# One wait ahead of a batch's DMA transposes, and two rectifications one slot later, in a fused attention and expert-layer kernel

## Chip, cores, metric

One core of one Trainium2 chip. The metric is the device time of one execution in microseconds (us), lower is better. The profile is one execution that the hardware profiler recorded; its span is about 1.7 us shorter than the time that the same execution is given (986.4 against 988.07 us for the kernel before). A run also has its mean *granted clock*: the share of full speed that the throttle allowed TensorE (PE).

## The reference, cut

Linear attention with cosine re-weighting, whose output goes through a router with eight rounds of balancing and eight experts.

```python
def phi(x, c, s):                      # c, s: cos and sin by position
    r = np.maximum(x, 0.0)
    return np.concatenate([r * c, r * s], axis=-1)
q_p, k_p = phi(q, ...), phi(k, ...)    # q, k, v: (8 batches, 8 heads, 576, 64)
kv  = einsum('bhsf,bhsd->bhfd', k_p, v);  z = k_p.sum(2)
num = einsum('bhsf,bhfd->bhsd', q_p, kv)
den = einsum('bhsf,bhf->bhs', q_p, z) + 1e-06
x   = (num / den)                      # then 4608 tokens x 512
# ... router, 8 rounds of balancing P, then for each of 8 experts:
out += P[:, e:e+1] * (np.maximum(x @ w1[e], 0) @ w2[e])
```

## The kernel before: the parts that matter

Expert 0 works on *blocks* of 512 tokens. A block has 16 *slots*: in slots 0 to 7 PE makes one part each of `h_ps` (x times w1), in slots 8 to 15 half a tile each of `y_ps` (h times w2). The attention of the coming batches is slipped in between: block `j` attends batch `j+1` and prepares batch `j+2`. Batches are counted from 0, so "the fourth batch" is `b == 3`, prepared in block 1. Each batch has four head pairs `hk`.

```python
ld      = tc.tile_pool(name="ld", bufs=4)        # q, k, v as loaded
qp_pool = tc.tile_pool(name="qp_pool", bufs=3)   # q_p before it is turned
ps_s    = tc.tile_pool(name="ps_s", bufs=4)      # small products, in PSUM
# ...
def load(b, half, names="qkv", held_back=False):
    for name in names:
        i = nc.gpsimd.dma_start(out=x, in_=...)  # 288 KB, two head pairs; float32 to fp16
        if held_back:
            after(ve.last, i)                    # not before what DVE was last given
        # ...
def prep_k(b, hk, by_scalar=True):               # rectifies k: ACT, in place
    se.activation(out=k16, in_=k16, func=AF.Relu)
def prep_q(b, hk):                               # b >= 2
    ve.tensor_scalar(out=q16, in0=q16, scalar1=0.0, op0=ALU.max)
    q_p = qp_pool.tile([P, C, 2, D], F16, name="q_p")
    ve.tensor_tensor(out=q_p, in0=q16, in1=cs, op=ALU.mult)
    nc.sync.dma_start(out=qTs[b, hk], in_=q_p, transpose=True)   # SyncE's queue
def prep_kv(b, hk):                              # DVE: k_p, then the copy of v
# ...
def attend(b, hk):       # PE: rb_ps; ACT: rb = copy(rb_ps); PE: num_ps; DVE: xT = num_ps * rb
# ... block 1 (j == 1), slot by slot:
#   0: loads of batch 3: second half of q, both of k, both of v (held back)
#   9, 10, 12, 13: attend(2, 0..3)
for slot, fn, hk in (                            # preparation of batch 3
    (4, prep_q, 0), (5, prep_q, 1), (7, prep_k, 0), (8, prep_q, 2),
    (8, prep_k, 1), (10, prep_kv, 0), (10, prep_k, 2), (12, prep_q, 3),
    (12, prep_kv, 1), (12, prep_k, 3), (13, prep_kv, 2), (14, prep_kp, 3),
    (14, prep_v, 3),
): ...
#   12: all six loads of batch 4 (held back);  15: key-value sums of batch 3, first half
#   block 2, slot 0: second half of those sums; slot 3: denominators, which need all four
#   transposed q of batch 3
```

PE, VectorE (DVE) and ScalarE (ACT) each work in written order, so an instruction that waits holds back everything behind it on its engine. The loads come from GpSimd's queue, the transposes from SyncE's.

## Time and profile before

| | before |
|---|---|
| time, median of 4 runs | 987.33 us (986.19 to 987.55) |
| profiled span, mean granted clock | 986.4 us, 0.996 |
| PE busy | 969.7 us, 98% |
| last `v` load of batch 3, issue to landing | 14.6 us |
| transposes of batch 3, issue to landing | 14.4, 15.1, 8.2, 3.2 us |
| PE idle from 57 to 70 us (waits with a releaser) | 4.5 us |

The page of the kernel before: the span, the engines' busy time, then three of its rows of 40 slices of 24.7 us each (PE's busy tenths, the granted clock, DMA's busy tenths).

```profile
span 986.4 us, 20270 instructions
...
PE 969.7 (98%) x7871; PEld 675.6 (68%) x7871; DVE 806.9 (82%) x1834; ACT 564.4 (57%) x1262; POOL 60.7 (6%) x82
...
PE   9989999989999999999999999999999999999997
...
PEclk9989999999999999999999999999999999999999
DMA  9999890642013410133113400133103401104535
...
```

PE is the bound nearly everywhere; the third slice (49 to 74 us) is the one in the attention part where PE shows an 8 and the granted clock an 8. In that slice DMA is at 9.

The waits of the kernel before, from 55 to 70 us: engine, line, tile, what it waited for, then us in total, times, longest.

```profile
...
engine line waited for: us in total, times, longest us
...
ACT k_ld L109 <- DMA k_ld<-in_k_dram: 6.6, 2, 4.9
DVE acc_lo L109 <- DMA v_ld<-in_v_dram: 5.1, 1, 5.1
PE small_ps L109 <- ACT rb L109: 4.1, 2, 3.0
...
```

ACT stood 4.9 us at a rectification whose `k` had not landed, DVE 5.1 us at a copy of `v`. Neither is PE, but PE writes its small products into four PSUM buffers (`ps_s`), and before the fourth attend those of the third come free only when ACT has copied `rb_ps` out, behind that rectification, and when DVE has made `xT`, behind that copy.

PE's timeline of the kernel before: start, us, instruction, and in brackets the idle time before it and what ended it.

```profile
...
start us, us, engine line op out<-in xcount [idle before <-releaser]
...
59.45 0.46 PE L109 MATMUL small_ps<-hl,acc_hi 96*128 96x192 f16 x3 [1.07 <-ACT rb L109]
...
62.96 1.04 PE L109 MATMUL y_ps<-w2e,hT 128*128 128x512 f16 x4
67.02 0.64 PE L109 MATMUL small_ps<-hl,acc_hi 96*128 96x192 f16 x3 [3.02 <-ACT rb L109]
68.05 0.69 PE L109 MATMUL small_ps<-q_pT,kv_sb 128*64 128x384 f16 x4 [0.39 <-DVE xT L109]
68.68 3.59 PE L109 MATMUL y_ps<-w2e,hT 128*128 128x512 f16 x8
72.20 1.17 PE L109 MATMUL small_ps<-acc_lo,k_p 64*128 64x65 f16 x36
...
74.50 0.74 PE L109 MATMUL small_ps<-acc_lo,k_p 64*128 64x65 f16 x36
...
```

The second attend waits 1.07 us, the fourth 3.02. After that gap the same work takes longer: eight `y_ps` matmuls take 3.59 us (1.90 elsewhere), 36 small ones 1.17 (0.74).

Why longer is in the view by windows: busy time of PE, weight loads, DVE, ACT and GpSimd, then the granted clock, the DMA share and GB/s.

```profile
...
core 0: us, PE busy (x) PEld busy (x) DVE busy (x) ACT busy (x) POOL busy (x), PEclk, DMA share, GB/s
64.00:67.00 3.00, 0.00 (x0) 0.00 (x0) 0.00 (x0) 1.57 (x4) 0.00 (x0) 0.99 1.31 135
67.00:70.00 3.00, 2.59 (x11) 1.14 (x11) 2.89 (x7) 2.42 (x6) 0.00 (x0) 0.50 1.09 154
70.00:74.00 4.00, 4.00 (x45) 1.85 (x44) 3.02 (x8) 1.02 (x3) 3.39 (x5) 0.53 0.80 104
...
```

From 64 to 67 us PE did nothing; from 67.0 to 73.8 its clock was half. The chain that ended last (start, us, what) runs through one load here:

```profile
...
53.23 13.82 DMA v_ld<-in_v_dram
...
67.45 0.56 DVE xT L109
...
68.05 0.69 PE small_ps L109 x4
...
```

### The profile page before, as it was taken

The numbers are of one execution on the slowest core, as the hardware profiler recorded it, in microseconds if no ns is written. First come the engines' busy times: TensorE is split into PE (matmuls) and PEld (weight loads), VectorE is DVE, ScalarE is ACT, GpSimd is POOL, SyncE is SP. The second block draws the span as 40 slices with busy tenths as digits, with TensorE's granted clock in tenths as the row PEclk, the third lists the DMA queues.
The fourth block names the chain that finished last, engine by engine and source line by source line (L and its number), as shares of the span: only waits on it lengthen the run. The fifth ranks groups of instructions, "written<-read, shape, count | busy, mean of one in ns | idle before, by whom it ended". The sixth has DMA issues, their size and how long they took to land.

```text
span 986.4 us, 20270 instructions
## 1 busy us (share of the span) xinstructions
PE 969.7 (98%) x7871; PEld 675.6 (68%) x7871; DVE 806.9 (82%) x1834; ACT 564.4 (57%) x1262; POOL 60.7 (6%) x82
## 2 busy tenths in 40 slices
PE   9989999989999999999999999999999999999997
PEld 6534545447777777777777777777777777777775
DVE  7766774789889888988789888988789888988887
ACT  5746665467776555555555555555555555555551
POOL 6222110010000000000000000000000000000001
PEclk9989999999999999999999999999999999999999
DMA  9999890642013410133113400133103401104535
GB/s 163 186 129 165 150 153 21 127 74 60 26 49 68 78 38 25 42 75 68 45 29 67 92 25 26 51 65 68 49 25 67 92 25 27 48 26 116 129 86 129
DMA packets 80336, 73.54 MB, mean 75 GB/s; under 512 B 33264, under 2 KB 72176, under 8 KB 80240
## 3 DMA queue, kind: packets, MB, share of 16 engines
q0 software_dynamic: 27232, 30.94, 20.3%
q1 hardware_dynamic: 52768, 41.06, 17.2%
q8 instruction: 61, 1.00, 0.4%
q14 instruction: 35, 0.29, 0.1%
q10 hardware_dynamic: 240, 0.26, 0.1%
HBM read 83.12 MB, written 12.98 MB: 97 GB/s over the span
## 4 chain that ended last, share of the span: by engine, by line
PE 90%; DMA 5%; issue 2%; DVE 2%; POOL 1%; ACT 1%; POOLq 0%; DVEq 0%; ACTq 0%; SPq 0%
PE rows_ps L109 34%; PE h_ps L109 27%; PE copied_ps L109 11%; PE p_ps L109 11%; PE y_ps L109 4%; PE small_ps L109 3%; DMA v_ld<-in_v_dram 1%; DMA w1e<-in_moe_w_dram 1%; DMA w2e<-in_moe_w_dram 1%; DMA k_ld<-in_k_dram 1%; POOL q_ld L201 0%; DVE acc_hi L922 0%; POOL hs_last L937 0%; DVE P_tok L109 0%; DMA out_dram<-acc_lo 0%
## 5 line engine op out<-in xcount | busy, mean ns | idle before, releaser
L922 DVE SCALAR_TENSOR_TENSOR acc_lo<-rows_ps,P_tok,acc_lo 128x512 f32<-128x512 f32 (+1 forms) x322 | 203.3, 640 | 74.4 <-PE rows_ps L109 74.3
L109 PEld LDWEIGHTS <-H 128*128 128x128 f16 x2080 | 203.0, 98 | 83.1 <-issue 1.2
L858 ACT CAST u<-h_ps 128x384 f16<-128x384 f32 x288 | 137.6, 478 | 131.2 <-PE h_ps L109 131.2
L109 PEld LDWEIGHTS <-w1e 128*128 128x128 f16 x1632 | 156.5, 98 | 66.6 <-issue 6.5
L852 DVE CUSTOM_DVE_ANT_0 H<-p_ps,u 128x384 f16<-128x384 f32 x329 | 181.1, 550 | 6.9 <-PE p_ps L109 6.5
L109 PEld LDWEIGHTS <-hs 128*128 128x128 f16 x1500 | 146.5, 98 | 56.2
L109 PE MATMUL h_ps<-S,w1e 128*128 128x384 f16 x672 | 164.1, 326 | 1.1 <-ACT u L109 0.9
L109 PE MATMUL p_ps<-xT,T 128*128 128x384 f16 x672 | 164.1, 326 | 0.1
L109 PE MATMUL rows_ps<-V,H 128*128 128x256 f16 x1000 | 150.0, 273 | 0.7 <-DVE acc_hi L922 0.7
L109 PE MATMUL h_ps<-xT,w1e 128*128 128x384 f16 (+1 forms) x616 | 150.2, 351 | 0.1
L109 PE MATMUL rows_ps<-w2e,hs 128*128 128x256 f16 x1000 | 150.0, 273 | 0.0
L890 ACT ACTIVATE H<-h_ps 128x384 f16<-128x384 f32 x144 | 70.6, 490 | 95.1 <-PE h_ps L109 95.1
L109 PEld LDWEIGHTS <-T 128*128 128x128 f16 x1008 | 98.1, 98 | 29.3 <-issue 2.8
L109 PE MATMUL rows_ps<-w2e,H 128*128 128x256 f16 (+1 forms) x568 | 91.2, 285 | 0.0
L871 ACT COPY copied_ps<-h_ps 128x384 f32<-128x384 f32 x144 | 67.5, 469 | 35.3 <-PE h_ps L109 35.3
L881 ACT ACTIVATE H<-copied_ps 128x384 f16<-128x384 f32 x144 | 70.9, 492 | 20.4 <-PE copied_ps L109 20.4
L109 PE MATMUL h_ps<-S,T 128*128 128x384 f16 x336 | 81.8, 325 | 0.3 <-ACT copied_ps L109 0.3
L109 PE MATMUL copied_ps<-xT,w1e 128*128 128x384 f16 x336 | 82.1, 326 | 0.0
L109 PE MATMUL copied_ps<-w2e,H 128*128 128x256 f16 x504 | 75.5, 272 | 0.0
L109 PE MATMUL rows_ps<-V,hs 128*128 128x256 f16 x500 | 74.9, 272 | 0.0
L922 DVE SCALAR_TENSOR_TENSOR acc_lo<-copied_ps,P_tok,acc_lo 128x256 f32<-128x256 f32 x126 | 60.1, 477 | 0.4
L922 DVE SCALAR_TENSOR_TENSOR acc_hi<-rows_ps,P_tok,acc_hi 128x512 f32<-128x512 f32 (+1 forms) x56 | 41.3, 737 | 20.5 <-PE rows_ps L109 19.7
(147 smaller groups left out, 953.5 us busy)
## 6 DMA issues: line engine op xcount, KB each, us to landing
S<-x_saved SPq DMA_DIRECT2D x108, 192.0 KB, 2.4
out_dram<-acc_lo SPq DMA_DIRECT2D x62, 128.0 KB, 2.4
w1e<-in_moe_w_dram POOLq DMA_DIRECT2D x7, 1024.0 KB, 9.1
w2e<-in_moe_w_dram POOLq DMA_DIRECT2D x7, 1024.0 KB, 9.6
q_ld<-in_q_dram POOLq DMA_DIRECT2D x16, 288.0 KB, 5.9
k_ld<-in_k_dram POOLq DMA_DIRECT2D x16, 288.0 KB, 8.0
v_ld<-in_v_dram POOLq DMA_DIRECT2D x16, 288.0 KB, 9.4
x_saved<-S SPq DMA_DIRECT2D x18, 192.0 KB, 1.9
```

Source lines behind the costliest of these rows:

```text
L109: i = getattr(self.engine, name)(*args, **kwargs)
L852: latest = ve._custom_dve(TENSOR_ADD_SAT, out=out, in0=ps[:, 0:TU], in1=t[:], s0=FP32_MAX, s1=0.0)
L858: se.copy(out=t[:], in_=ps[:, 0:TU])
L871: se.copy(out=Y[:, 0:TU], in_=X[:, 0:TU])
L881: se.activation(out=h11, in_=Y[:, 0:TU], func=AF.Relu)
L890: se.activation(out=h12, in_=X[:, 0:TU], func=AF.Relu)
L922: ve.scalar_tensor_tensor(out=a, in0=rows, scalar=P_tok[:, g, self.e : self.e + 1], in1=a, op0=ALU.mult, op1=ALU.add,)
```

## The change

The intent: let the loads of batch 3 have the DMA engines for themselves, by keeping its transposes back until the last `v` has landed; and let ACT rectify the first two `k` one slot later, so that a late `k` doesn't stand ahead of an attend's `rb`.

```diff
+        landing = {}
 # ... in load():
+                landing[name, b, half] = i
 # ... in prep_q():
-                nc.sync.dma_start(
+                turned = nc.sync.dma_start(
                     out=qTs[b, hk], in_=..., transpose=True,
                 )
+                if b == 3 and hk == 0:
+                    after(landing["v", b, 1], turned)
 # ... block 1:
-                    (4, prep_q, 0), (5, prep_q, 1), (7, prep_k, 0), (8, prep_q, 2),
-                    (8, prep_k, 1), (10, prep_kv, 0), (10, prep_k, 2), (12, prep_q, 3),
+                    (4, prep_q, 0), (5, prep_q, 1), (8, prep_k, 0), (8, prep_q, 2),
+                    (9, prep_k, 1), (10, prep_kv, 0), (10, prep_k, 2), (12, prep_q, 3),
```

## The prediction

> **What bounds the kernel now.** TensorE: the page shows PE busy 98% of a 986.4 us span, and PE lines fill 90% of the chain that ended last. The change touches one stretch, 50 to 75 us, where batch 3 (the fourth) is loaded and prepared while the products of the second token block run.
>
> The chain of waits, in that window, runs through one transfer: v_ld, issued 53.23, 13.82 us to landing. The timeline shows its cost: PE idles 1.07 us at 58.4 and 3.02 at 64.0 (released by ACT rb) and 0.39 at 67.7; ACT sat 4.92 us for k_ld, DVE 5.08 us for v_ld, with PE's next operands (rb, xT) behind those instructions. Then the granted clock, by stretches of 1 us, is 0.50 from 67.0 to 73.8: 6.8 us at half speed cost about 3.4 (8 y_ps matmuls took 3.59 us there, 1.90 elsewhere). The Trainium skill ("TensorE: Matmul & The Clock Gate", Part 1, What's actually happening) has the clock halve after an idle window of about 3.4 us; this trace agrees: 64.0 to 67.0 has no matmul. Together 4.5 idle + 3.4 slow = about 7.9 us at stake.
>
> **Why the loads are late.** Second halves of k and v, issued 52.5 to 53.9, landed at 65.4, 67.1, 68.5. Batch 3's transposes (SyncE queue), issued 52.3, 54.1 and 62.0, took 14.4, 15.1 and 8.2 us; alone they take 3.2 to 3.4. From 57 to 62 the load queue moved 54 to 99 KB per us, against 170 just before and 205 alone. So the two kinds slow each other; the skill ("DMA: Bandwidth & Descriptors", Issuing engines are not separate DMA queues) says that they share the same 16 engines and interleave.
>
> **What the change does.** (1) All four batch-3 transposes wait for the last v load (three stand behind the first in SyncE's order). Loads then land every 1.43 us, as in later batches: k about 57.1 and 58.5, v about 60 and 61.5, 7 us sooner. (2) The first two rectifications of k (0.68 us each on ACT) move one slot later, so rb of the first attend is no longer behind both: that 1.07 us wait shrinks to about 0.4.
>
> **What it costs.** The transposes start at about 61.6; the first lands about 65. q_p has three buffers, so the fourth prep_q on DVE must wait for it, about 1.5 to 2 us at 63.3, with the second k_p, v copy and the last xT behind. PE then waits about 1.0 us before the key-value sums (about 66.8 instead of 72.2) and about 0.9 before the second ones (about 69.2 instead of 74.5). Transposes must be in by the denominators, about 72.5; the last lands about 69.3.
>
> **Sum.** About 2.0 to 2.3 us less PE idle, plus 3.4 for the half-clock stretch, which should vanish, as no idle gap comes near 3 us: 5.3 us, all on the critical path. 987.1 - 5.3 = about 982 us, range 980.0 to 984.5. Faster by over 2%: 1%; within 2%: 97%; slower: 2%.
>
> **What would show it.** k and v of batch 3 landing 5 to 9 us after issue; transposes issued after the last v, 3.2 to 5 us each; no clock below 1.0 between 60 and 80 us; PE gaps of about 1 us between 64 and 70; DVE idle before the fourth q_p, released by a DMA; the second key-value sums near 69 us.
>
> **What would make it wrong.** Loads slow for another reason (v lands after 63); the q_p wait grows past 3 us and halves the clock again (gain 1 to 2 us); batch 4's loads collide with the late transposes; or the q_p wait doesn't come (gain near 7).

## The result, and the profile after

| | before | after |
|---|---|---|
| median of the runs | 987.33 us (986.19 to 987.55, 4 runs) | 983.34 us (982.04 to 985.58, 4 runs) |
| ratio, 95% interval | 1 | 0.9964 (0.9944 to 0.9984) |
| profiled span, clock | 986.4 us, 0.996 | 980.3 us, 0.999 |

A ratio here is the mean time of one kernel's fast runs over that of the other's of the same rounds, so not quite the ratio of the medians that are quoted. By it the change is worth 0.36%, about 3.6 us; by the 2% measure the two are the same. The two profiled executions differ more: that of the kernel before took 988.07 us, more than any of its four runs above, and that of the changed kernel 982.04, its fastest.

The page after: span, engines, and the row of the granted clock.

```profile
span 980.3 us, 20270 instructions
...
PE 967.1 (99%) x7871; PEld 674.9 (69%) x7871; DVE 806.6 (82%) x1834; ACT 564.3 (58%) x1262; POOL 60.6 (6%) x82
...
PEclk9999999999999999999999999999999999999999
...
```

The 8 in the third slice of the clock is gone, and PE's busy time fell by 2.6 us with the same number of matmuls: they ran at full clock.

PE's timeline after:

```profile
...
start us, us, engine line op out<-in xcount [idle before <-releaser]
...
58.68 0.46 PE L109 MATMUL small_ps<-hl,acc_hi 96*128 96x192 f16 x3 [0.23 <-ACT rb L109]
...
63.06 0.41 PE L109 MATMUL small_ps<-hl,acc_hi 96*128 96x192 f16 x3
63.40 0.44 PE L109 MATMUL small_ps<-q_pT,kv_sb 128*64 128x384 f16 x4
63.77 1.90 PE L109 MATMUL y_ps<-w2e,hT 128*128 128x512 f16 x8
65.60 0.74 PE L109 MATMUL small_ps<-acc_lo,k_p 64*128 64x65 f16 x36
...
67.50 0.46 PE L109 MATMUL small_ps<-acc_lo,k_p 64*128 64x65 f16 x18 [0.18 <-DVE acc_lo L109]
68.16 0.46 PE L109 MATMUL small_ps<-acc_lo,k_p 64*128 64x65 f16 x18 [0.21 <-DVE k_p L109]
...
72.39 0.35 PE L109 MATMUL small_ps<-acc_hi,zsel 128*32 128x192 f16 x6 [0.46 <-DMA acc_hi<-q_p]
...
```

The 3.02 us gap is gone (the fourth attend, at 63.06, waits for nothing), the eight `y_ps` matmuls take 1.90 us again, and the second part of the key-value sums ends at 68.62 (68.16 + 0.46) instead of 75.24 (74.50 + 0.74): 6.6 us sooner. The last line is new: PE waits 0.46 us for a transpose.

The windows after, the same stretches:

```profile
...
core 0: us, PE busy (x) PEld busy (x) DVE busy (x) ACT busy (x) POOL busy (x), PEclk, DMA share, GB/s
64.00:67.00 3.00, 3.00 (x48) 1.51 (x46) 3.00 (x7) 2.04 (x6) 1.01 (x2) 1.00 0.93 177
67.00:70.00 3.00, 2.61 (x45) 1.37 (x44) 1.76 (x7) 1.40 (x4) 3.00 (x5) 1.00 0.95 115
70.00:74.00 4.00, 3.54 (x38) 1.66 (x36) 1.19 (x2) 1.68 (x4) 0.30 (x1) 1.00 1.26 221
...
```

The chain after, where that new wait lies; before, the chain of the same stretch went through `v_ld`, now it goes through the fourth transpose, which took 6.26 us to land:

```profile
...
66.08 6.26 DMA acc_hi<-q_p
...
72.39 0.35 PE small_ps L109 x6
...
```

6.6 less 0.5 is the 6.1 us by which the two profiled spans differ. Of the 6.6, less idle PE is 3.9 (4.48 before, 0.23 + 0.18 + 0.21 after). The clock is the rest, 2.4 us by another count: from the fourth attend's `num_ps` to the end of the second sums PE took 7.2 us without a wait (68.05 to 75.24) and 4.8 after, waits taken off (63.40 to 68.62, less 0.39).

**What the order of the queue shows.** The compiler is free to reorder a DMA queue, and did. Rows 6 to 9 of SyncE's order in the compiled program, before and after (names are shortened; one ending in 267 is head pair 0's buffer, 268 is head pair 1's):

```
before: 6 DmaTranspose q_pT_267   7 DmaTranspose q_pT_268   8 ... acc_lo   9 ... acc_hi
after:  6 DmaTranspose q_pT_268   7 DmaTranspose q_pT_267 [waits for the v load]   8 ... acc_lo   9 ... acc_hi
```

Only head pair 0's transpose has the wait, and head pair 1's was put ahead of it. It went out at 53.76 us, in the midst of the loads. So of the three transposes that shared the window before, one still does. Issue and landing, from the records of the DMA issues (us from the span's start, time to landing in parentheses):

```
                 before                     after
k, second half   52.52 -> 65.41 (12.89)     52.51 -> 59.21 ( 6.70)
v, first half    53.23 -> 67.06 (13.82)     53.22 -> 61.38 ( 8.16)
v, second half   53.94 -> 68.52 (14.58)     53.93 -> 63.17 ( 9.24)
1st transpose    52.32 -> 66.68 (14.36)     53.76 -> 63.80 (10.04)   head pair 1
2nd transpose    54.09 -> 69.18 (15.08)     63.19 -> 66.48 ( 3.29)   head pair 0
3rd transpose    62.03 -> 70.21 ( 8.18)     64.59 -> 67.88 ( 3.29)
4th transpose    69.44 -> 72.67 ( 3.23)     66.08 -> 72.34 ( 6.27)
1st load, b. 4   70.61                      65.99
```

The fourth transpose went out at nearly the same moment as the first of six loads of batch 4. That is the 0.46 us, and it is where the rest of this story lies.

### The profile page after: what moved, and what is told of

Read it like the earlier page. It is cut to its first block, busy times and chain, and to the rows that moved or that the text cites. A ratio compares the mean times of both kernels' runs of the same rounds, so it can differ in the third digit from the quotient of the medians.

```text
span 980.3 us, 20270 instructions
## 1 busy us (share of the span) xinstructions
PE 967.1 (99%) x7871; PEld 674.9 (69%) x7871; DVE 806.6 (82%) x1834; ACT 564.3 (58%) x1262; POOL 60.6 (6%) x82
## 4 chain that ended last, share of the span: by engine, by line
PE 94%; DVE 2%; ACT 2%; DMA 1%; POOL 0%; issue 0%; ACTq 0%; SPq 0%; POOLq 0%
PE rows_ps L109 34%; PE h_ps L109 28%; PE copied_ps L109 11%; PE p_ps L109 11%; PE y_ps L109 6%; PE small_ps L109 4%; DMA acc_hi<-q_p 1%; ACT hT L109 0%; ACT acc_lo L109 0%; DVE acc_hi L927 0%; POOL hs_last L942 0%; DVE P_tok L109 0%; DMA out_dram<-acc_lo 0%; DVE colp L109 0%; ACT u L109 0%
## 5 line engine op out<-in xcount | busy, mean ns | idle before, releaser
L109 PE MATMUL copied_ps<-w2e,H 128*128 128x256 f16 x504 | 75.5, 272 | 0.0
```

The source lines that it names most:

```text
L109: i = getattr(self.engine, name)(*args, **kwargs)
```

## The experiments

The theory: loads and transposes in flight together slow each other; three transposes in the load window delay `k` and `v` until PE runs dry, and the dry stretch halves the clock. Rivals: ACT's order is what held PE; the halved clock costs nothing, as PE would wait anyway; any wait will do. Each run below was timed in five rounds against the kernel before on the same chip. "Full clock" is a run with a mean granted clock of 0.999 or 1.000 (every trace ends with a few us at half clock, whatever came before).

### The changed kernel, twice more

No edit. The first:

> The changed kernel once more, for a second trace and more times. If the 6.1 us that its first profiled run gained over the kernel before is the rule, the median is 981 to 983 us; if the scatter of its first four runs (982.0 to 985.6) is its own, the median stays near 983.3 with single runs up to 985.6.

Measured: 983.4 us median, six runs 982.70 to 989.10, ratio 0.9979 (0.9958 to 0.9999). The second reading held: the scatter is the kernel's own. Clock and time go together: four runs at full clock are 982.70 to 983.68, the other two 986.24 (0.998) and 989.10 (0.996).

The last run:

> The changed kernel a third time, to count how often it still loses the clock. So far 3 of its 10 runs lie at a mean clock of 0.998 or less (985.6 to 989.1 us) and 7 at 0.999 or 1.0 (982.0 to 983.7). Theory (one transpose still shares the window with the loads, so the loss is rarer, not gone): again 1 to 3 of 6 runs at 985 us or more, the rest at 982 to 984; with all four waiting for the first half of v none of 6 did. Rival (those were chance): none of 6.

Measured: 983.48 us median, ratio 0.9968 (0.9946 to 0.9991); two of six runs at a lower clock, 985.90 and 986.79, the other four 982.65 to 983.77. As the theory had it. This time the profiled execution was one of the bad ones (span 985.1), so it shows where the time went. PE's waits there from 50 to 90 us, and the window in which the clock fell:

```profile
...
PE small_ps L109 <- DMA acc_hi<-q_p: 2.0, 1, 2.0
PE small_ps L109 <- ACT rb L109: 1.4, 1, 1.4
...
```

```profile
...
74.00:78.00 4.00, 2.43 (x14) 1.07 (x14) 1.96 (x3) 0.60 (x1) 0.00 (x0) 0.86 1.16 177
...
```

PE waited 2.0 us for the fourth transpose (7.77 us to landing; the loads of batch 4 were issued from 67.64, it at 67.76), and the clock was halved for 3.4 us from 76.9. So what the change still loses, it can lose at a new place: a transpose of batch 3 under the loads of batch 4.

### The two parts by themselves

```diff
 # wait_only: the changed kernel with the old slots
-  (8, prep_k, 0), ... (9, prep_k, 1)
+  (7, prep_k, 0), ... (8, prep_k, 1)
 # slots_only: the kernel before with the new slots
```

> The wait alone, k rectified in the old slots. Theory (transposes and loads fight for the DMA engines; the wait frees the loads): keeps nearly all of the gain, 0.5 to 1 us slower than the changed kernel, because rb of the first attend is again behind two rectifications (PE wait near 58.5 us about 1.0 instead of 0.2). No half clock between 60 and 80 us. Rival (ACT's order is what held PE): within 2 us of the kernel before.

> The slot move alone, no wait. Theory: v of batch 3 still lands at about 67 us, PE still idles about 3 us from 64 and the clock still halves for 6.8 us, so the time is that of the kernel before within 1 us (986 to 987.6), though the 1.07 us wait at 58.4 shrinks. Rival (ACT's order is what held PE): 983 to 985 us.

Measured: the wait alone 983.07 us (982.42 to 984.59), ratio 0.9966 (0.9954 to 0.9977); the slots alone 987.77 us (987.58 to 989.22), ratio 1.0015 (1.0003 to 1.0027), clock 0.998 or less in all five runs. The kernel with the wait alone was not slower than the changed one: that part of the expectation missed. The slots alone, waits from 55 to 70 us:

```profile
...
DVE acc_lo L109 <- DMA v_ld<-in_v_dram: 6.9, 1, 6.9
PE small_ps L109 <- ACT rb L109: 5.3, 2, 4.7
...
```

`v` was as late as ever, PE's waits for `rb` are still 5.3 us in all, with one of 4.7. The first rival falls. The wait is the change; the slot move is worth nothing that these runs show. It did shorten PE's wait at the second attend (1.07 us before, 0.57 with the slots alone, 0.23 after), but not reliably: when `k` landed at 59.0 instead of 57.1 us, that wait was 2.07 us in the first repeat of the changed kernel, slots and all.

### More waits, fewer waits

```diff
 # all_wait
-                if b == 3 and hk == 0:
+                if b == 3:
 # third_waits
-                if b == 3 and hk == 0:
+                if b == 3 and hk >= 2:
```

> All four transposes of batch 3 carry the wait, so that the compiler cannot put the second one ahead of the first, as it did in the changed kernel (SyncE's order shows q_pT of head pair 1 first, without the wait, issued 53.8 us). This is the kernel that the prediction described: loads land 1.43 us apart (v at about 60 and 61.5), no transpose in flight between 54 and 61 us, the first lands near 65, DVE waits about 1.5 to 2 us for it before the fourth q_p, PE about 1 us before each of the key-value sums. Theory: 0.5 to 1.5 us slower than the changed kernel, still 3.5 us or more faster than before. Rival (any transpose in the load window costs more than the q_p wait): faster than the changed kernel.

> The wait sits on the third and fourth transposes of batch 3 only, so two transposes share the window with the loads (three in the kernel before, one in the changed kernel, none with all four waiting). Theory (each transpose in the window delays the loads): the last v lands 11 to 13 us after its issue, between the 9.2 to 10.1 of one transpose and the 14.6 to 15.8 of three; PE idles about 1 to 2 us before the third attend; 983.5 to 986 us, some runs with the clock halved. Rival (the load window is free as soon as any wait is there): 9 us, time of the changed kernel.

Measured, all four waiting: 983.68 us (983.32 to 984.32), ratio 0.9968 (0.9955 to 0.9981); every run at full clock. Issue order as written. The last `v` took 8.45 us, no transpose before 63.29. DVE waited 2.3 us before the fourth `q_p`, PE 1.5, 0.3 and 0.2 us before the key-value sums, as the prediction had said for the changed kernel. It is as fast as the changed kernel in the median, and its five runs have none of the bad ones; five are few.

Measured, the third and fourth waiting: 986.34 us, ratio 0.9982 (0.9959 to 1.0006), in two heaps: 981.76 and 982.02 at full clock, four runs of 985.29 to 988.56 at 0.998 or less. The profiled execution was a lucky one, and there the last `v` took 10.0 us with two transposes beside it, less than the 11 to 13 expected. So the traces don't grade the delay by the number of transposes. The share of bad runs hints at it (table below), on few runs; the interval of the ratio includes 1 and overlaps that of the changed kernel, so the last rival, that any wait will do, is not settled by this run. Which runs are lucky stays open too: a trace of both heaps was not taken.

### The clock by itself

```diff
 # the kernel before, plus, at block 1, slot 12 (clock_kept) or slot 13 (clock_kept_13):
+        def fill():
+            f_ps = ps_h[0].tile([P, TCH], FP32, name="h_ps")   # nobody reads it
+            for _ in range(12):                                # 14 in clock_kept_13
+                te.matmul(out=f_ps[:], lhsT=ones_sq[:], rhs=..., start=True, stop=True)
```

> The kernel before, with twelve matmuls of ones (about 0.22 us each, 2.6 us together) put into TensorE's order just ahead of the third attend, where it sits idle for 3 us; nothing reads them. Loads, transposes and waits stay as they are. Theory (the idle gap halves the clock, and that is a cost of its own): no clock below 1.0 between 60 and 80 us in any run, time 984 to 986, that is 1.5 to 3 us faster than the kernel before, as its own full-clock runs are (984.2 to 986.3). Rival (the halved clock is hidden by the late loads): same as before within 0.7 us.

Measured: 988.47 us, ratio 1.0008 (0.9994 to 1.0023), two of six runs at full clock. The expectation missed, and the edit was wrong: the 3 us gap is ahead of the fourth attend, the fill went ahead of the third. PE's timeline of it:

```profile
...
62.56 2.77 PE L109 MATMUL h_ps<-ones_sq 128*128 128x512 f16 x12
...
65.88 1.04 PE L109 MATMUL y_ps<-w2e,hT 128*128 128x512 f16 x4
67.99 0.46 PE L109 MATMUL small_ps<-hl,acc_hi 96*128 96x192 f16 x3 [1.08 <-ACT rb L109]
69.22 0.69 PE L109 MATMUL small_ps<-q_pT,kv_sb 128*64 128x384 f16 x4 [0.76 <-DVE xT L109]
69.84 3.11 PE L109 MATMUL y_ps<-w2e,hT 128*128 128x512 f16 x8
...
```

The fill (62.56) is followed by the third attend and, after 65.88 + 1.04, by gaps of 1.08 and 0.76 us. No gap was near 3 us, yet the clock was halved from 68.9 for 3.4 us. That is the most useful thing that this failed run gave (see the end).

> The kernel before with fourteen unread matmuls (3.0 us) ahead of the fourth attend of batch 2, which is where the 3 us gap really is; the run before this put them one attend too early, ahead of the third, and the clock still halved. Loads and transposes as before. Theory (the halved clock is a cost of its own, 2.4 us in place): no halved clock between 60 and 80 us in at least most runs, 984.5 to 986 us. Rival (the late loads cover it): 987 us or more.

Measured: 986.1 us (985.66 to 988.89), ratio 1.0014 (0.9991 to 1.0037). The clock was full in five of six runs, as meant, and the profiled one (span 984.0) shows none halved between 60 and 80. But the time is no better than that of the kernel before: five full-clock runs have a mean of 986.2 us, against 986.9 for the seven runs of before below 0.999 in the same rounds, and 982.8 for its four at full clock. Both expectations missed. The fill takes its 3.2 us of PE also in runs whose loads are on time, so what lucky runs gain may be lost with it, and the times don't separate the two. The trace does: its last `v` landed at 67.95 us, nearly as late as in the kernel before, but the clock stayed full.

```profile
...
67.24 0.54 PE L109 MATMUL small_ps<-q_pT,kv_sb 128*64 128x384 f16 x4
...
71.97 0.46 PE L109 MATMUL small_ps<-acc_lo,k_p 64*128 64x65 f16 x18 [0.21 <-ACT hT L109]
...
```

From the fourth attend's `num_ps` to the end of the second sums PE took 5.0 us there, the wait taken off (67.24 to 72.43, less 0.21), against 7.2 in the kernel before. So the halved stretch cost 2.2 to 2.4 us in place, by three traces; that a whole run is shorter by it is not shown.

### Taking DVE's wait away

With all four waiting, the largest loss left is DVE's 2.3 us for a `q_p` buffer. Two ways of being rid of it:

```diff
 # q3_later: all_wait, and
-  (12, prep_q, 3), (12, prep_kv, 1), ... (14, prep_v, 3)
+  (12, prep_kv, 1), ... (14, prep_v, 3), (14, prep_q, 3)
 # all_wait_4q: all_wait, and
-  qp_pool bufs=3, rb_pool bufs=4
+  qp_pool bufs=4, rb_pool bufs=3
```

> All four transposes wait, and the fourth q_p of batch 3 is made two slots later, behind the k_p, v copies and the last xT on DVE, so that DVE's wait for the first transpose (2.3 us with all four waiting) holds back nothing. Theory: the PE waits of 1.5 and 0.3 us before the key-value sums go; about 1.5 us faster than with all four waiting: 981.5 to 982.5 us, every run at full clock. The last transpose must still land before the denominators at about 72 us. Rival (the q_p wait costs nothing): 983.7 us as before.

> All four transposes wait, q_p has four buffers instead of three (and rb three instead of four, to make room), so the fourth q_p waits for no transpose of its own batch. Theory: as with the later q_p, 981.5 to 982.5 us at full clock; DVE's 2.3 us wait for a transpose gone. rb with three buffers may give back some tenths by ACT waits for DVE.

Measured: 994.39 us, ratio 1.0077 (1.0061 to 1.0092), and 993.41 us, ratio 1.0065 (1.0051 to 1.0079). Both were to be the fastest; both are slower than the kernel before. DVE's wait is gone in both, as intended. PE's waits with four `q_p` buffers:

```profile
...
PE small_ps L109 <- DMA acc_lo<-q_p: 7.0, 1, 7.0
PE small_ps L109 <- DMA acc_hi<-q_p: 2.9, 1, 2.9
```

The loads of batch 4 are held back behind DVE's work of slot 12. While DVE waited for a transpose, so did they. With the wait gone they went out at 65.25 (68.81 with all four waiting), on top of the third and fourth transposes, which took 12.24 and 13.84 us instead of 3.38 and 3.25. The denominators need all four. With the later `q_p` it is the fourth that took 13.09 us, and PE waited 9.8 us for it; the clock was then at half for 13.7 us. If that is the cause, holding the loads must bring it back:

```diff
 # gated_4q: all_wait_4q, and in load()
+                if b == 4:
+                    after(turnings[2], i)      # the third transpose of batch 3
```

> The kernel with four q_p buffers and all four transposes waiting (993.4 us), with one thing more: the six loads of batch 4 wait until the third transpose of batch 3 has landed. Theory (that kernel lost its 10 us because, with DVE's wait gone, batch 4's loads were issued 3.5 us sooner and fell on the last two transposes, which took 12 to 14 us instead of 3.3): the last transpose lands within 4.5 us of its issue, before 72 us, the PE waits of 7.0 and 2.9 us for them vanish, and the time is 981 to 983 us. Rival (fewer rb buffers or the other order cost the 10 us): stays above 990 us.

Measured: 985.27 us (983.36 to 987.52), ratio 0.9994 (0.9970 to 1.0019). The transposes took 3.24 to 3.42 us, PE's waits for them are gone, and 8 us came back by the medians (7 by the ratios; the two were timed on different chips): the cause is shown, and the three `rb` buffers are not it. But 981 to 983 was missed: now batch 4 is late. ACT waits up to 4.1 us for its `k`, PE 2.7 us for `rb` at 78 us, and half of the runs lose some clock there.

### All four wait, but for the first half of v

```diff
 # all_wait_v0: all_wait, and
-                    after(landing["v", b, 1], turned)
+                    after(landing["v", b, 0], turned)
```

> All four transposes wait, but for the first half of v instead of the second; q_p keeps three buffers. Theory: the first transpose starts 1.4 us sooner and shares the engines with one load for about 1.4 us; DVE's wait for it (2.3 us) shrinks to about 1 us, batch 4's loads still come after the last transpose; 0.7 to 1.5 us faster than with all waiting for the last v (983.7): 982.2 to 983 us, clock full in every run. Rival (the overlap with the last load stretches both): no faster, 983.7 or more.

Measured: 982.13 us, six runs from 981.70 to 982.88, all at full clock; ratio 0.9969 (0.9947 to 0.9990). The first transpose went out at 60.73 and landed in 3.38 us beside the last load (8.21 us); DVE waited 0.9 us; the fourth transpose went out at 65.11, ahead of the first load of batch 4 at 66.30, and took 3.39. All of PE's waits from 50 to 90 us:

```profile
...
PE small_ps L109 <- DVE acc_lo L109: 0.3, 1, 0.3
PE small_ps L109 <- ACT rb L109: 0.3, 1, 0.3
PE small_ps L109 <- DVE k_p L109: 0.2, 1, 0.2
```

The kernel before had its most good runs in those rounds (four of eleven at full clock), so the ratio is no better than the changed kernel's and doesn't rank the two. The spread, 1.2 us over six runs against 7.1 over the changed kernel's sixteen, speaks for this version, but six runs on one chip don't show that it is the better one.

### All together

"In window" counts the transposes of batch 3 issued before the last `v` landed; landings, waits and spans are of the profiled execution, PE's waits are those from 55 to 85 us. The two clock_kept kernels are left out.

| kernel | in window | last v, us to landing | 4th transpose, us | PE waits, us | runs at full clock | median us |
|---|---|---|---|---|---|---|
| before | 3 | 14.6 | 3.2 | 4.5 | 10 of 43 | 986.9 |
| slots_only | 3 | 15.8 | 3.2 | 5.9 | 0 of 5 | 987.8 |
| third_waits | 2 | 10.0 | 3.3 | 1.1 | 2 of 6 | 986.3 |
| after (three traces) | 1 | 9.2, 10.1, 10.7 | 6.3, 5.4, 7.8 | 1.1, 2.1, 3.9 | 11 of 16 | 983.4 |
| wait_only | 1 | 9.4 | 6.9 | 1.9 | 5 of 6 | 983.1 |
| all_wait | 0 | 8.5 | 3.3 | 2.5 | 5 of 5 | 983.7 |
| all_wait_v0 | 1, at its end | 8.2 | 3.4 | 0.8 | 6 of 6 | 982.1 |
| all_wait_4q | 0 | 8.8 | 13.8 | 9.9 | 0 of 6 | 993.4 |
| q3_later | 0 | 8.1 | 13.1 | 10.7 | 0 of 6 | 994.4 |
| gated_4q | 0 | 9.1 | 3.2 | 3.7 | 3 of 6 | 985.3 |

The line of the kernel before pools its runs (one run, 1428.71 us, is left out). Over those 43 runs its full-clock ones have a mean of 983.9 us and the rest 987.2; the changed kernel's 16 have 983.0 and 986.7. So the two kernels differ less within a class (0.9 and 0.5 us) than in how often they fall into the good one: 23% and 69%. With the old share, the changed kernel's class means would give 985.9 (10/43 of 983.04 and 33/43 of 986.72); with its own share they give 984.2. Of the 2.3 us between the means of all runs (986.5 and 984.2) about 0.6 is within the classes and 1.7 is the share. "Class" is a description: in the traces of bad runs, the idle gap and the lost clock come together. The rounds differ, too: on the four chips the kernel before was at full clock in 3 of 10, 0 of 11, 4 of 11 and 3 of 11 runs, and third_waits, all_wait_4q and q3_later were timed where it was never so. So shares of kernels from different rounds are compared with care.

## Why the prediction was right, and where it was off

Predicted 982.0 us (980.0 to 984.5), within 2%; measured 983.34. The direction and the size class were right, and so was the main mechanism, that the loads land sooner once transposes are kept out of their way: shown by the wait alone against the slots alone. That the number came so near is partly luck. In the first pair of traces PE's idle time fell by 3.4 us (4.48 to 1.08) where 2.0 to 2.3 was said, the clock gave 2.4 where 3.4 was said, and neither comes in full in every run.

- *The load window.* Right: the wait that takes transposes out of it has all of the gain, without the slot move. Mis-sized: "Loads then land every 1.43 us", the last `v` at 61.5. With no transpose of batch 3 in flight it landed at 62.2 to 63.2 (8.1 to 9.1 us from issue), as the loads landed 2.84, 0.95 and 1.37 us apart in all_wait, not 1.43 each.
- *"PE's next operands (rb, xT)".* Wrong, without harm to the sum: the engine that PE waits for is right, but PE reads no `rb`. It waited for PSUM buffers of the attend before, which ACT empties by copying `rb_ps` and DVE by making `xT`.
- *"(three stand behind the first in SyncE's order)".* Wrong. The wait sits on one transpose, and the compiler put the next one ahead of it. The sentence described another kernel, all_wait, and that one behaved as written: 2.3 us of DVE wait where 1.5 to 2 was said. In the changed kernel DVE waited 0.51 us and PE 0.4 before the sums (1.9 was said), so the profiled execution gained 6.1 us where 5.3 was predicted.
- *"3.4 for the half-clock stretch, which should vanish, as no idle gap comes near 3 us".* This is the step that failed. In place the halved clock was worth 2.2 to 2.4 us, not 3.4. And it vanished in 11 of 16 runs, not in all: in the third trace a gap of 2.0 us was enough (PE busy 1.42 us in the 3.41 us before the halving). A gap of 2.07 us in the second trace was not; it fell across two windows of that length, with PE busy 2.26 and 2.36 us in them. The median gained 3.6 to 4 us and not the 6.1 of the first traces, which pair a bad run of the one kernel with the best of the other.
- *"The last lands about 69.3".* It landed at 72.3, 72.6 and 75.5 in three traces, because the loads of batch 4, sooner too, fall on it. The prediction named that collision as a way to be wrong; it happened in all three, and PE waited 0.5, 0 and 2.0 us for it.
- *The slot move.* "That 1.07 us wait shrinks to about 0.4": 0.23 in the first trace, 2.07 and 1.4 in the other two. No time came of it.

What stays open: what decides whether one execution is lucky (the kernel before had runs of 982.0 us on one chip), and what the lost clock costs a whole run apart from the gap that lowers it.

## What to carry to other kernels

Order transfers by who needs them first, and see that two kinds of them don't meet: a wait that kept one kind back was worth more here than the engine time it cost. Before removing a wait, ask what else it was holding back; here DVE's wait for a buffer was what kept the next loads off the transposes. And when runs of one kernel scatter, sort them by granted clock before comparing: a change may move few microseconds in each class and many runs from one class to the other. Put a wait on every instruction that must obey it, since a queue's written order is not a promise.

## What the Trainium skill lacked or had wrong

- "TensorE: Matmul & The Clock Gate" (Part 1, What's actually happening) has the clock halve after an idle window of about 3.4 us, and its section "Why this matters for your kernels" asks for no PE-idle gaps over about 3 us. The period agrees: here the halved stretches are 3.41, 6.83, 10.24 and 13.65 us long. But the window need not be idle. In the 3.41 us window before a halving PE was busy 0.44 us in the kernel before, 1.42 in the changed kernel's third trace (longest gap 2.0 us) and 1.88 in clock_kept (longest gap 1.08 us). No border comes out of these traces: counted in steps of 3.41 us from the halvings of the same trace, windows with 1.96 us busy (all_wait, from 65.08 us) and even 1.63 us (in the last 7 us of all_wait, all_wait_v0 and clock_kept) had no halving at their end.
- "DMA: Bandwidth & Descriptors" (Rules for kernel authors) says that a transpose next to ordinary DMAs needs nothing. The row is about corrupted data, and all runs were correct. For time it doesn't hold: alone, a transpose of 128 x 1152 fp16 took 3.2 to 3.4 us; under loads up to 16 us, while the last of the loads took 14.1 to 15.9 us with three transposes beside them and 8.1 to 9.1 with none. The page's "Issuing engines are not separate DMA queues" says that they share 16 engines and interleave, which agrees; no page has the size of it.
- No page that was read says that the compiler may reorder DMAs of one queue around a wait. It did here: head pair 1's transpose went out at 53.76 us, the first one, with the wait, at 63.19. It was reordered when the program was built, not by the hardware.
